# A fused spectral-mixing and SwiGLU kernel in fp32: gate and value as 4x2 by 2x4 block products with sums put into PSUM banks

## The chip, the cores and the metric

One core of one Trainium2 chip. The metric is the device time of one execution in microseconds (us). Profiled executions add a trace; engines are written PE (TensorE), PEld (its weight loads), DVE (VectorE), ACT (ScalarE), POOL (GpSimd) and SP (SyncE).

## The reference

```python
# x: (8, 3008, 256), filt_r/filt_i: (1505, 256), all fp32
X = np.fft.rfft(x, axis=1)
y = np.fft.irfft(X * (filt_r + 1j * filt_i), n=3008, axis=1)   # spectral mixing
x = y.reshape(24064, 256)
g = x @ w_gate                          # 256 -> 1536
silu = g / (1 + np.exp(-g))
out = (silu * (x @ w_val)) @ w_out      # 1536 -> 256
```

The spectral part is done as matrix products too (stages 1, 2 and 3 of a factored Fourier transform). While the hidden layer of batch b runs, the spectral stages of batch b+1 are slipped in between its products.

## The kernel before

The hidden layer is cut into 192 pieces: 8 batches, 4 chunks of tokens, 6 blocks of hidden columns. In each piece gate and value are each a 2x2 by 2x2 block product made with 7 block products in place of 8. The seven results are put together by copies out of PSUM (ACT), additions (DVE), and products that add onto a bank.

```python
def step(z, p):                         # z: gate or value, p: which of 7 products
    ...
    if p in (1, 6, 7):
        product(z, p, "A", p == 1)      # 376 columns, two records for one fp32 product
        nc.scalar.copy(out=u[(1, 6, 7).index(p)], in_=bk[z]["A"])
    ...
    elif p == 2:
        product(z, p, "F")
        add(nc.vector, dst[z][:, 0], u[0], bk[z]["F"])      # one operand in SBUF, one in PSUM
    ...                                 # (silu and multiply: cut)

e = nc.gpsimd                           # the four sums that the projection needs
add(e, h[:, 4], h[:, 1], h[:, 2])
sub(e, h[:, 5], h[:, 0], h[:, 1])
sub(e, h[:, 1], h[:, 4], h[:, 0])
sub(e, h[:, 6], h[:, 3], h[:, 1])
```

The weights of gate and value, rounded and summed once, stay in SBUF for the whole run (`wg_t`, `wv_t`).

## Time and profile before

| | before |
|---|---|
| time, median of all its runs beside the change | 3118.78 us (3118.35 to 3119.38, 4 runs) |
| profiled span | 3116.7 us |
| PE's budget (each record at its own pace) | 2992.6 us |
| loss before the first hidden product (which stands at 104.9 us) | 69.5 us |
| loss from there to 0.3 ms ("start") | 31.6 us |
| loss from 0.3 ms to 40 us before the end ("steady") | 15.5 us |
| loss in the last 40 us and after the last matmul's start ("end") | 7.4 us |

A loss is worked out from the trace like this: the distance from the start of one matmul record to the start of the next, less the pace of that form of record (0.112 us for 94 or 128 columns, 0.159 for 188, 0.216 for 256, 0.316 for 376, 0.430 for 512). It says where TensorE stood still or ran late, whatever made it. A lower granted clock is inside it. The warm-up products are not in the budget, so they count as loss before the first hidden product.

### The profile page before, as it was taken

The page shows a single profiled execution, that of the slowest core. Times are in us where ns is not written, and L with a number is a line of the kernel's source. Part 1 is how long each engine was busy: PE and PEld are TensorE (multiplying, and loading weights), DVE is VectorE, ACT ScalarE, POOL GpSimd, SP SyncE. Part 2 cuts the span into 40 slices and gives each one's busy share as a digit, 9 for nine tenths or more (in the row PEclk, how much of TensorE's full clock was granted, in tenths as well). Part 3 has the DMA queues.
Part 4 walks back from the last instruction along what each step waited for, and adds up shares of the span by engine and source line. Part 5 has one row for each costly group of instructions (what it writes and reads, how often), then busy time and mean ns, then how long its engine had stood idle before and what let it go on. Part 6 is the DMA issues. An engine that isn't in the chain of part 4 may idle for free.

```text
span 3116.7 us, 41163 instructions
## 1 busy us (share of the span) xinstructions
PE 3056.4 (98%) x15560; PEld 2240.5 (72%) x15560; DVE 1476.5 (47%) x2348; ACT 1140.3 (37%) x2070; POOL 1405.8 (45%) x1622
## 2 busy tenths in 40 slices
PE   7789999999999999999999999999999999999999
PEld 4457777777767777767777777767777677777776
DVE  4664553354543554345543455434553444544443
ACT  0443333333343343343333333343333433333333
POOL 3574454444543444444543454434544344533343
PEclk8999999999999999999999999999999999999999
DMA  8432222222212222222222132121322222200000
GB/s 233 130 117 68 72 81 56 61 76 68 75 55 72 59 79 60 61 68 81 69 60 65 57 88 71 51 71 55 91 68 56 63 63 68 68 28 21 21 6 16
DMA packets 123634, 212.51 MB, mean 68 GB/s; under 512 B 23670, under 2 KB 69750, under 8 KB 122578
## 3 DMA queue, kind: packets, MB, share of 16 engines
q1 hardware_dynamic: 91692, 132.25, 14.8%
q0 software_dynamic: 24448, 68.71, 7.7%
q10 hardware_dynamic: 7296, 8.92, 1.1%
q8 instruction: 123, 2.02, 0.3%
q14 instruction: 75, 0.61, 0.1%
HBM read 134.81 MB, written 74.97 MB: 67 GB/s over the span
## 4 chain that ended last, share of the span: by engine, by line
PE 80%; POOL 7%; DVE 6%; issue 3%; DMA 2%; ACT 2%; SPq 0%; POOLq 0%; ACTq 0%; DVEq 0%
PE wA_v L435 15%; PE wA_g L435 15%; PE wA_o L499 7%; PE wE_v L435 7%; PE wE_g L435 7%; PE wE_o L499 7%; PE wF_o L499 4%; PE wF_g L435 4%; PE pd L396 3%; PE wF_v L435 3%; POOL o L162 3%; PE pa L332 3%; POOL h L165 3%; PE pc L376 2%; PE pb L356 2%
## 5 line engine op out<-in xcount | busy, mean ns | idle before, releaser
L435 PE MATMUL wA_v<-y,wv_t 128*128 128x376 f32 x1536 | 612.5, 480 | 7.3 <-ACT u_v L444 4.3
L435 PE MATMUL wA_g<-y,wg_t 128*128 128x376 f32 x1536 | 614.3, 481 | 4.4 <-POOL wg_t L229 3.5
L165 POOL TENSOR_TENSOR h<-h 128x376 f32<-128x376 f32 x576 | 566.9, 984 | 28.8
L162 POOL TENSOR_TENSOR h<-h 128x376 f32<-128x376 f32 x192 | 188.4, 981 | 701.2 <-PE wE_v L435 389.1
L444 ACT COPY u_g<-wA_g 128x376 f32<-128x376 f32 x576 | 269.5, 468 | 589.9 <-PE wA_g L435 587.6
L435 PEld LDWEIGHTS wA_v<-y,wv_t 128*128 128x128 f32 x1536 | 289.2, 190 | 204.0 <-DVE h L457 15.6
L499 PEld LDWEIGHTS wA_o<-wo_t,h 128*128 128x128 f32 x3456 | 406.3, 192 | 16.3
L499 PE MATMUL wA_o<-wo_t,h 128*128 128x128 f32 x3456 | 417.5, 275 | 0.0
L435 PEld LDWEIGHTS wA_g<-y,wg_t 128*128 128x128 f32 x1536 | 281.1, 190 | 172.3 <-issue 28.1
L462 ACT ACTIVATE s<-s 128x1128 f32<-128x1128 f32 x192 | 219.5, 1143 | 373.2 <-DVE s L162 373.2
L464 DVE TENSOR_TENSOR h<-s,h 128x1128 f32<-128x1128 f32 x192 | 257.1, 1339 | 124.0 <-ACT s L462 124.0
L435 PE MATMUL wE_g<-y,wg_t 128*128 128x376 f32 x768 | 307.1, 482 | 2.1 <-DVE s L162 2.1
L435 PE MATMUL wE_v<-y,wv_t 128*128 128x376 f32 x768 | 306.1, 480 | 1.8 <-DVE h L162 1.6
L444 ACT COPY u_v<-wA_v 128x376 f32<-128x376 f32 x576 | 272.2, 473 | 69.3 <-PE wA_v L435 65.2
L162 DVE TENSOR_TENSOR s<-u_g,wE_g 128x376 f32<-128x376 f32 x384 | 208.9, 544 | 176.2 <-ACT u_g L444 174.6
L162 DVE TENSOR_TENSOR s<-u_g,wF_g 128x376 f32<-128x376 f32 x192 | 104.4, 544 | 394.9 <-PE wF_g L435 369.3
L499 PE MATMUL wE_o<-wo_t,h 128*128 128x128 f32 x2304 | 281.6, 276 | 7.5 <-DVE o L162 7.5
L499 PE MATMUL wF_o<-wo_t,h 128*128 128x128 f32 x2304 | 278.5, 275 | 0.0
L499 PEld LDWEIGHTS wE_o<-wo_t,h 128*128 128x128 f32 x2304 | 267.4, 192 | 13.6 <-DVE o L162 13.6
L499 PEld LDWEIGHTS wF_o<-wo_t,h 128*128 128x128 f32 x2304 | 267.8, 192 | 0.3
L162 POOL TENSOR_TENSOR p<-p,q 128x512 f32<-128x512 f32 x96 | 121.6, 1266 | 226.4 <-DVE q L367 226.4
L162 DVE TENSOR_TENSOR h<-u_v,wE_v 128x376 f32<-128x376 f32 x384 | 208.9, 544 | 26.5 <-ACT u_v L444 5.1
(86 smaller groups left out, 3275.3 us busy)
## 6 DMA issues: line engine op xcount, KB each, us to landing
t<-d SPq DMA_DIRECT2D x192, 128.0 KB
t<-d SPq DMA_DIRECT2D x64, 384.0 KB
d<-t POOLq DMA_DIRECT2D x112, 192.0 KB, 2.5
tb<-de_tbl SPq DMA_DIRECT2D x84, 256.0 KB
d<-g POOLq DMA_DIRECT2D x168, 128.0 KB, 2.8
x<-in_x_dram SPq DMA_DIRECT2D x112, 160.0 KB
out_dram<-o POOLq DMA_DIRECT2D x128, 128.0 KB, 2.0
f<-in_filt_r_dram SPq DMA_DIRECT2D x168, 64.0 KB
```

Source lines behind the costliest of these rows:

```text
L162: eng.tensor_tensor(out=dst, in0=a, in1=b, op=ALU.add)
L165: eng.tensor_tensor(out=dst, in0=a, in1=b, op=ALU.subtract)
L332: nc.tensor.matmul(out=ps[0:NK], lhsT=wf_t, rhs=self.x.pop(u), start=True, stop=True)
L356: nc.tensor.matmul(out=ps[:, i, :], lhsT=self.tb[u][:, i, 0, :], rhs=t2[:, i, :], start=True, stop=True)
L376: nc.tensor.matmul(out=ps[:, i, :], lhsT=tb[:, i, 1, :], rhs=pt[:, i, :], start=True, stop=True)
L396: nc.tensor.matmul(out=psv[:, n, :], lhsT=self.t4[k, i][:, n, ts(cb, 128)], rhs=wi_t, start=True, stop=True)
L435: nc.tensor.matmul(out=bk[z][kind], lhsT=wt[z][:, j, LEFT[p], :], rhs=y[:, RIGHT[p], :], start=start, stop=True, skip_group_check=True)
L444: nc.scalar.copy(out=u[(1, 6, 7).index(p)], in_=bk[z]["A"])
L462: nc.scalar.activation(out=s[:, 0:3], in_=s[:, 0:3], func=AF.Silu)
L464: nc.vector.tensor_tensor(out=h[:, 0:3], in0=s[:, 0:3], in1=h[:, 0:3], op=ALU.mult)
L499: nc.tensor.matmul(out=bk[kind][:, t, :], lhsT=hs[i][:, HID[p], t0:t0 + 128], rhs=wo_t[:, JB * q + i, WO[p], :], start=start and t == 0 an ...
```

## The change

Intent: TensorE is the bound, so fewer products should give a shorter run. Two former pieces become one group, 96 in all. Its gate and value are a 4x2 by 2x4 block product made with 26 products in place of 32 (28 before), of 188 columns each. What the scheme has to add up goes partly *into* PSUM ahead of a product: DVE writes a sum of two SBUF tiles into a bank and the product adds onto it. The weights no longer fit, so each group's weights come from DRAM while the group before it runs. One long list fixes the order of every operation on every engine.

```diff
-LEFT = {1: 0, 2: 1, 7: 2, 4: 3, 5: 4, 6: 5, 3: 6}
-RIGHT = {1: 0, 2: 1, 3: 2, 4: 3, 5: 4, 6: 5, 7: 6}
+SCHEDULE = """
+Q0 n1' h0' Q1 S21' f0 P3 o3' f1 t4.3' t0.0 f3 P1 x0' t0.1 P0 x1' Q2 d1 x2' c0 W1 S00' x3' c1 f2
+t0.2 x4' s01 S10' Q3 s13 x5' o1 c3 A01 A13 m01 t1.0 S31' m13 s03 S20' s23 P2 y13 t1.1 B01 t0.3 d2
+A03 u01 A23 c2 t1.2 m03 s02 B13 m23 y12 W6 u13 y23 A02 t2.0 e13 o6 e03 m02 S30' E13 t2.1 t1.3 B03
+l13 B23 u03 s12 E03 e12 y01 u23 B02 e02 l03 A12 u02 n3 t2.2 E12 m12 E02 t2.3 l12 e23 t3.0 l02 n2
+W7 t3.1 E23 o7 W2 e01 l23 g1 t3.2 E01 o2 W5 t3.3 l01 h1 t4.0 B12 o5 t4.1 W4 S01 u12 g0 W3 S11 t4.2
+o4
+""".split()
+BY_POOL = ("01", "12", "13", "23")
 ...
-    wg_t = cpool.tile([128, NJ, 7, 128], FP32)
-    wv_t = cpool.tile([128, NJ, 7, 128], FP32)
+    wt_t = cpool.tile([128, NPR, 2, 128], FP32)          # one group's 26 x 2 weight blocks
+    w_dram = wdpool.tile([NG, 128, NPR, 2, 128], FP32, name="w_all")
 ...
+    def reload_weights(g, piece):
+        a, b = PIECES[piece]
+        tc.keep_in_program_order(nc.sync.dma_start(out=wt_t[:, a:b], in_=w_dram[g, :, a:b]))
 ...
+            elif kind == "s":        # a sum put into a bank, ahead of product A
+                pin(add(v, self.bank(f"a{at}"), t[f"q{i}"], t[f"p{j}"]))
+            elif kind in "AB":       # the product adds onto it
+                self.product(op, f"a{at}", False)
+            elif kind == "y":
+                if at in BY_POOL:
+                    pin(add(nc.gpsimd, self.small(f"y{at}", 3), self.place(i, i), self.place(j, j)))
+            elif kind == "e":
+                if at in BY_POOL:
+                    pin(act.mul(self.bank(f"e{at}"), t[f"y{at}"], -1.0))
+                else:
+                    pin(negated_sum(self.bank(f"e{at}"), self.place(i, i), self.place(j, j)))
+            elif kind == "l":
+                pin(sub(v, self.place(j, i), t[f"e{at}"], t[f"m{at}"]))
+            elif kind == "S":        # sums for the projection, as before on POOL
+                h = self.hs[j]
+                dst, a, b, f = ((4, 1, 2, add), (7, 4, 0, sub), (5, 0, 1, sub), (6, 3, 7, sub))[i]
+                pin(f(nc.gpsimd, h[:, dst], h[:, a], h[:, b]))
 ...   (spectral stages cut in parts, rounding by half blocks, warm-up: cut)
```

In the list P, Q, A, B and E are products, `s` and `e` sums put into banks, `f`, `d`, `c`, `m`, `u` and `l` what leaves them, `y` and `S` sums on POOL, `g` silu, `h` the multiply, `W`, `o` and `x` the projection with its output, `n` the sums of the sequence blocks for the next group, `t` a part of a spectral stage. A prime marks work of an earlier group.

## The prediction

> **What bounds the kernel now.** I read the page's busy shares first, then TensorE's waits, then its timeline in the middle of the run.
>
> ```profile
> PE 3056.4 (98%) x15560; PEld 2240.5 (72%) x15560; DVE 1476.5 (47%) x2348; ACT 1140.3 (37%) x2070; POOL 1405.8 (45%) x1622
> ```
>
> Busy TensorE (PE) time of pipelined matmuls can hide gaps, so this alone proves little. The list of PE's waits (us in total, times, longest) is short:
>
> ```profile
> PE pc L376 <- POOL p L162: 9.2, 10, 1.8
> PE pa L332 <- DVE t L336: 8.0, 5, 3.8
> PE wE_o L499 <- DVE o L162: 7.5, 32, 0.7
> PE wA_v L435 <- ACT u_v L444: 4.3, 4, 2.7
> ```
>
> The timeline (start us, busy us, then the instruction and how many stand together) gives the pace:
>
> ```profile
> 1003.37 0.80 PE L435 MATMUL wA_v<-y,wv_t 128*128 128x376 f32 x2
> 1004.00 0.80 PE L435 MATMUL wF_v<-y,wv_t 128*128 128x376 f32 x2
> 1004.63 1.02 PE L332 MATMUL pa<-x,wf_t 94*96 94x512 f32 x2
> 1005.49 0.80 PE L435 MATMUL wA_g<-y,wg_t 128*128 128x376 f32 x2
> ```
> ```profile
> 1500.64 2.17 PE L499 MATMUL wA_o<-wo_t,h 128*128 128x128 f32 x18
> 1502.65 2.17 PE L499 MATMUL wE_o<-wo_t,h 128*128 128x128 f32 x18
> ```
>
> Each fp32 product is two matmul records. Start to start, a 376-column product takes 0.63 us (0.316 a record), a 512-column one 0.86 (0.430), and 18 projection records 2.01 (0.112 each). The 256-column records follow each other every 0.216 us, the 94-column ones (pd) every 0.112. The busy columns (0.48 us a record) overlap; only these distances count. From 0.4 ms to the end the distances have almost no excess. So PE's issue rate is the bound, and its budget is: hidden 5376 x 0.316 = 1699; projection 8064 x 0.112 = 903; spectral stages 256 x 0.430 + 768 x 0.216 + 1024 x 0.112 = 391; sum 2993 us. The other 124 us of the 3117 are mostly the first 0.3 ms, as the stage table shows (window, length, busy us of PE, PEld, DVE, ACT, POOL, clock, DMA share, GB/s):
>
> ```profile
> 55.00:95.00 40.00, 30.11 (x97) 20.93 (x98) 33.05 (x48) 6.88 (x12) 15.87 (x14) 0.80 0.59 154
> 95.00:105.00 10.00, 9.09 (x27) 4.43 (x25) 0.00 (x0) 0.95 (x2) 0.00 (x0) 0.94 0.60 160
> 105.00:165.00 60.00, 43.61 (x140) 21.75 (x141) 44.49 (x68) 30.38 (x52) 46.18 (x52) 0.94 0.42 129
> 165.00:300.00 135.00, 130.55 (x673) 94.86 (x672) 73.58 (x119) 55.34 (x102) 72.87 (x86) 0.98 0.28 85
> 1000.00:2900.00 1900.00, 1895.01 (x9794) 1404.80 (x9793) 893.23 (x1424) 710.05 (x1291) 851.39 (x978) 1.00 0.22 63
> ```
>
> The first gate product stands at 104.9 us, and weight preparation delays PE until about 0.3 ms.
>
> **What the Trainium skill says.** "TensorE: Matmul & The Clock Gate", section "Back-to-back issue gap", gives a warm distance of N/2.4 + 2.5 ns; "FP8 and Floating Point Precision", "TensorE Precision Notes", says true fp32 takes four passes. Two passes in each record give 2 x 376/2.4 + 2.5 = 315.8 ns; the trace has 316. The first page's section "LDWEIGHTS" puts a 128-column weight load at 107 ns however narrow the rest; the trace agrees in that 94 and 128 columns cost the same 112 ns. "PSUM — Partial Sum Buffer", "The four PSUM rules", says VectorE's writes do not change the bits that decide whether a matmul adds or overwrites; that is why the new kernel can put a sum in a bank and let a product add onto it, after dummy matmuls set those bits. Nothing in the kernel before shows that.
>
> **The change, part by part.**
>
> 1. Hidden products. Before, 7 for 8: 14 products of 376 columns for each of 192 pieces. After, 96 groups (each of two former pieces), with 26 products of 188 columns for both gate and value: 96 x 26 x 2 x 2 = 9984 records. The dangerous question is whether a short matmul is still paid by column. The line through 256 (216 ns) and 512 (430) gives 0.159 us at 188, clearly above the 0.112 floor, so weight loading does not bind: 9984 x 0.159 = 1590 us. This saves **109 us**. Had the floor bound them the gain would be negative, so this is the first thing to check.
> 2. Projection (8064 records) and spectral stages (same counts) stay: 0. PE's budget becomes 1590 + 903 + 391 = 2884, or 30.0 us a group.
> 3. DVE per group, from rows of before: the 376-column adds are 0.544 us, SBUF multiply 1.34 at 1128 columns, so 1.73 at 1504. Sixteen adds and subtractions on banks and halves 8.8, two multiplies 3.5, 5.7 output adds of 0.554 3.1, the sequence sums 1.7, spectral products (now three operations of 0.69 for four) 2.1, stage-3 copies 0.5: 19.7 of 30 us, 65% against 47% before. Not the bound, but far less loose.
> 4. ACT per group: 24 evictions of 0.47 = 11.3, two silus of 1.5 = 2.9, spectral copies 2.1, output copies 0.6, DMA issues 3.3 x 0.48 = 1.6: 18.5 us, 62%. POOL: 12 operations of 0.98, one addition of 1.27, two output issues of 0.58: 14.2 us, 47%.
> 5. Weights now come from DRAM for every group: 26 x 2 x 128 x 128 x 4 bytes = 3.4 MB in 30 us, 114 GB/s on top of some 65. The first 55 us moved 255 GB/s, so 180 fits. Each piece has about 20 us between its last use and its next. Hidden.
> 6. The start. In place of one column block, three or four must be ready before a group flows. All four steps of stage 3 now share one bank, each waiting for a copy of 0.8 to 1.0 us: +5 us. The third weight block is rounded behind nine sequence sums: about +11 before the third product. Then step 0 holds twelve half-roundings and six weight sums on DVE. From the before trace I estimate 2.15 us for one half (five operations, 3.56 us at double width), so 26 + 6 + the group's 11 = 43 us of DVE against 21 us of PE; step 1 has 17 + 6 + 15 = 38 against 30. Lost: 22 + 8 + 14 (with the first weights) + some 4 of friction = 48 us, against about 36 lost before at this place. First product at 112 instead of 105.
> 7. The end. The last group's multiply, five POOL sums and seven projection parts run alone: some 8 us after PE's budget is used up, 6 before.
>
> Sum: 112 to the first product, then 2884 less what of batch 0's spectral work is done by then (38) = 2846, start losses 48, end 8, and about 10 of small waits as before: 3024. To that I add 11 for new steady waits (below): **3035 us**.
>
> **Rivals.**
> (a) *The fixed order makes PE wait in every group.* Walking through the schedule with these durations, most producers finish over 1 us early. The tight place is the chain silu, multiply h0, output add, spectral products, sum s01, product A01 at the start of a group: only about 0.4 us early, and late by about 0.9 where the sequence sums n1 come first and the group begins with a spectral stage 2 (two groups of a batch, 14 us in all). For it speaks DVE at 65% in strict order; against it that the author placed everything by hand. Each 0.1 us a group costs 10 us: at 0.4 us a group the time is some 3060, at 1 us 3115 and the gain is gone.
> (b) *DVE becomes the bound.* It would need 30 us a group; I count 20. Were its operations slowed by POOL's sharing (the rounding's tensor-scalar takes 0.43 us alone and 0.70 beside POOL), it might be 23. No for the steady state, yes for the first two steps.
> (c) *Reloads collide with spectral loads* on one in-order queue, so that stage 1 or 2 waits: a few us a group at worst, 3050 to 3150. Against: the queue issues an item in 0.42 us, some 15 a group, and transfers average under 25% busy.
> (d) *The saving is bigger*, if PE has no new wait and the start is no worse: 2884 + 124 = 3008.
>
> **Range and chances.** 3005 (rival d) to 3080 (rival a at 0.6 us a group). The 2% line is 3057, 22 us above my value, i.e. 0.23 us more a group than I assume; I give 0.77 to faster, 0.21 to within 2%, 0.02 to slower.
>
> **What would show it.** Distances of 0.159 us between 188-column records confirm step 1; anything near 0.19 breaks it. PE's waits should be dominated by the first 0.25 ms; a list with hundreds of waits on DVE sums (wa) or ACT evictions means rival a; waits of spectral products on DMA mean c. DVE should read about 65% and ACT 60%; over 80% means b. The first product should stand near 112 us, and the table of stages should show PE idle for 40 to 55 us between there and 0.25 ms. The prediction is wrong if steady groups take over 30.5 us.

## More of the kernel before

The rounding of one weight block is a chain over three engines; only its shape matters here:

```python
v.tensor_scalar(out=man, in0=high, ...)                      # DVE
nc.scalar.activation(out=w, in_=man, ...)                    # ACT
v.tensor_scalar(out=pw, in0=high, ...)                       # DVE
nc.scalar.activation(out=pw, in_=pw, func=AF.Relu, ...)      # ACT
v.tensor_scalar(...); v.scalar_tensor_tensor(...); v.scalar_tensor_tensor(...)   # DVE
e.tensor_tensor(out=dst[...], in0=w, in1=pw, op=ALU.mult)    # POOL; frees w and pw
```

The DVE groups by form in the kernel before (line, engine, operation, output and inputs, shapes, count; then total busy us and mean ns; then idle time before them):

```profile
L464 DVE TENSOR_TENSOR h<-s,h 128x1128 f32<-128x1128 f32 x192 | 257.1, 1339 | 124.0 <-ACT s L462 124.0
L162 DVE TENSOR_TENSOR s<-u_g,wE_g 128x376 f32<-128x376 f32 x384 | 208.9, 544 | 176.2 <-ACT u_g L444 174.6
...
L162 DVE TENSOR_TENSOR o<-o,wF_o 128x384 f32<-128x384 f32 x64 | 35.5, 554 | 174.6 <-PE wF_o L499 161.8 <-POOL o L162 12.8
```

See what the operands are. In the second and third lines one input is a PSUM bank (wE_g and wF_o are banks, u_g and o are SBUF tiles). Only the multiply in the first line reads two SBUF tiles.

## The result

| | before | after |
|---|---|---|
| median (range, runs) | 3118.78 us (3118.35 to 3119.38, 4) | 3233.93 us (3230.89 to 3241.42, 4) |
| ratio, with 95% interval | | 1.0373 [1.0355, 1.0391], slower |
| profiled span | 3116.7 | 3229.1 |
| PE's budget | 2992.6 | 2881.3 |
| loss before the first hidden product | 69.5 | 73.4 |
| loss, start | 31.6 | 108.1 |
| loss, steady | 15.5 | 148.8 |
| loss, end | 7.4 | 17.6 |

A ratio is the mean time of one kernel's fast runs over the mean of the other's in the same rounds, so it is not quite the ratio of the medians.

The budget fell by 111 us as meant. The losses rose by 224: 77 in the start, 133 in the steady part, 10 at the end and 4 before the first product. The busy line of the changed kernel's page:

```profile
PE 2994.4 (93%) x20124; PEld 2849.8 (88%) x20124; DVE 2223.4 (69%) x3198; ACT 1568.9 (49%) x3002; POOL 1558.8 (48%) x1586
```

No engine is full, and PE fell from 98% to 93%. The pace of the new products, from TensorE's timeline in the middle of the run (start us, busy us, instruction, how many together):

```profile
1526.95 2.71 PE L584 MATMUL wa<-y_t,wt_t 128*128 128x188 f32 x16
1529.50 1.17 PE L657 MATMUL wA<-wo_t,h 128*128 128x128 f32 x9
```

Sixteen records in 2.55 us are 0.159 us each: a 188-column record is paid by its columns. So the loss is waiting. PE's waits after the change (total us, times, longest):

```profile
PE wa L584 <- DVE wa L199: 84.1, 44, 13.4
PE pa L436 <- DMA x<-in_x_dram: 25.7, 6, 5.0
PE wk L584 <- ACT q L598: 21.6, 4, 7.9
PE wpb L458 <- DMA t<-d: 16.1, 1, 16.1
```

The first line is the product onto a sum, waiting for DVE's sum: the rival (a) of the prediction, though in 44 waits and not in every group. Seven of them, 45 us, lie before 0.32 ms. The second line, six waits of about 4.3 us, is stage 1 without its input. The third is one wait early in each of the first four groups; the last of them ends at 312 us. The fourth line lies before the first hidden product. The stages (window, length, busy us of PE, PEld, DVE, ACT, POOL, clock, DMA share, GB/s):

```profile
112.00:165.00 53.00, 19.18 (x51) 13.98 (x50) 30.71 (x80) 12.32 (x30) 17.62 (x35) 0.56 0.42 139
165.00:300.00 135.00, 87.32 (x476) 78.21 (x475) 94.66 (x185) 59.91 (x123) 70.18 (x99) 0.79 0.42 137
1000.00:2900.00 1900.00, 1842.09 (x12636) 1771.28 (x12635) 1329.92 (x1850) 970.63 (x1844) 920.80 (x903) 0.99 0.57 179
```

In the first two stages no engine is busy much over 70% of the time, DVE included. That is a chain of latencies rather than a full engine. The clock there is 0.56 and 0.79 where before had 0.93 and 0.98 in the same windows; in the steady window it is 0.99 against 1.00.

The part of the loss that is the lower clock itself can be read from the traces. Take the records that follow the one before them without a wait of over 0.15 us. Those issued while the granted clock was under 0.95 stand 1.97 times their pace apart (median). From 0.32 ms to 40 us before the end, this excess makes 29 us of the loss after the change, and none before it; it is 15 us in x_early and none in s_on_dve and sum_parts, runs told below. Between the first product and 0.32 ms it makes 24 us, and 4 before the change. What lowers the clock is not shown: half_on_dve and pool_free stand idle for 111 and 100 us in the steady stretch with only 3 and 5 us of this excess.

**The sum that costs twice its price.** DVE's groups by form after the change:

```profile
L199 DVE TENSOR_TENSOR wa<-q,p 128x376 f32<-128x376 f32 x576 | 581.7, 1042 | 11.9
...
L202 DVE TENSOR_TENSOR h<-we,m 128x376 f32<-128x376 f32 x576 | 315.1, 548 | 303.1 <-PE we L584 298.9 <-ACT h L625 0.5
```

Same shape, same count. The `l` operation in the second line reads a bank and a tile and takes 548 ns, as the sums of the kernel before did. The `s` operation in the first line reads two SBUF tiles, q and p, and takes 1042 (581.7/576 gives 1.01 us). Sorted by what POOL does meanwhile, after 0.25 ms, the 148 of these sums that no POOL operation overlaps take 550 ns, and the 416 others have a median of 1291. The length goes with the number of POOL operations that overlap a sum: the medians are 812 ns beside one, 1237 beside two and 5532 beside six. The worst case, one of six such sums, in DVE's timeline and then POOL's at the same time:

```profile
1208.15 0.55 DVE L206 SCALAR_TENSOR_TENSOR p<-wk,q 128x376 f32<-128x376 f32 x1
1208.81 5.53 DVE L199 TENSOR_TENSOR wa<-q,p 128x376 f32<-128x376 f32 x1
```

```profile
1208.92 1.26 POOL L199 TENSOR_TENSOR p<-p,q 128x512 f32<-128x512 f32 x1
1210.15 0.97 POOL L199 TENSOR_TENSOR y<-h,h 128x376 f32<-128x376 f32 x1
1211.09 0.96 POOL L199 TENSOR_TENSOR y<-h 128x376 f32<-128x376 f32 x1
1212.02 0.97 POOL L202 TENSOR_TENSOR h<-h 128x376 f32<-128x376 f32 x1
1212.95 0.96 POOL L199 TENSOR_TENSOR y<-h 128x376 f32<-128x376 f32 x1
```

POOL is in the middle of an operation when the sum starts (it began at 1207.66). The sum then stays on DVE while five more POOL operations go through one behind the other, and ends 0.43 us after the last of them (1213.91 to 1214.34), somewhat less than the 0.55 that it takes alone. TensorE pays at once:

```profile
1214.49 1.12 PE L584 MATMUL wa<-y_t,wt_t 128*128 128x188 f32 x4 [2.51 <-DVE wa L199]
```

The Trainium skill has this: "SBUF — State Buffer", section "Who interferes with whom", says that a DVE instruction with two SBUF inputs contends with a GpSimd instruction that reads SBUF, that the lock is exclusive, and that who issues first decides. The trace agrees that the two contend (550 against 1291 ns). It does not show issue order deciding: five POOL operations that started after the sum went ahead of it. The prediction does not cite this page.

**Input behind the reloads.** SP's timeline, the issue of transfers in order:

```profile
930.98 39.98 SPq L323 DMA_DIRECT2D wt_t<-w_all  x7
971.01 0.89 SPq L361 DMA_DIRECT2D t<-d  x2
971.95 4.02 SPq L361 DMA_DIRECT2D x<-in_x_dram  x6
```

and TensorE's, soon after:

```profile
979.76 2.02 PE L436 MATMUL pa<-x,wf_t 94*96 94x512 f32 x2 [4.56 <-DMA x<-in_x_dram]
```

A reload may start only when the last product that reads the old block is through. SP waits for that, as the list of SP's waits says (total us, times, longest):

```profile
SPq L323 <- PE wa L584: 1368.3, 253, 10.0
SPq L323 <- PE wk L584: 592.6, 88, 16.7
```

What stands behind the reload in SP's program waits with it: x is issued at 971.95 and lands too late.

**The start.** TensorE's timeline in the first group:

```profile
133.96 5.38 PE L584 MATMUL wk<-y,wt_t 128*128 128x188 f32 x16 [5.95 <-ACT q L598]
152.46 1.62 PE L584 MATMUL wa<-y_t,wt_t 128*128 128x188 f32 x4 [13.12 <-DVE wa L199]
```

and DVE's, at the seam of two half-roundings and then at a later one:

```profile
118.75 0.43 DVE L273 SCALAR_TENSOR_TENSOR pw<-raw,pw 128x256 uint32<-128x256 uint32 x1
121.09 0.29 DVE L262 TENSOR_SCALAR w<-raw 128x256 uint32<-128x256 uint32 x1 [1.92 <-POOL wt_t L199]
...
146.72 0.29 DVE L262 TENSOR_SCALAR w<-raw 128x256 uint32<-128x256 uint32 x1 [5.47 <-DMA raw<-in_moe_w_gate_dram]
```

Each half uses the same two buffers, so DVE stands still until POOL has finished the half before (0.3 to 1.9 us, in about half of the roundings after the first product), and later until the next raw weights land. The product's sum is behind this in DVE's order.

### The profile page after: what moved, and what is told of

Its sections match the earlier page's. It is cut to its first block, busy times and chain, and to the rows that moved or that the text cites. A ratio compares the mean times of both kernels' runs of the same rounds, so it can differ in the third digit from the quotient of the medians.

```text
span 3229.1 us, 54700 instructions
## 1 busy us (share of the span) xinstructions
PE 2994.4 (93%) x20124; PEld 2849.8 (88%) x20124; DVE 2223.4 (69%) x3198; ACT 1568.9 (49%) x3002; POOL 1558.8 (48%) x1586
## 4 chain that ended last, share of the span: by engine, by line
PE 79%; DVE 11%; DMA 5%; issue 2%; POOL 2%; ACT 1%; SPq 1%; ACTq 0%; POOLq 0%; DVEq 0%
PE wa L584 22%; PE wA L657 13%; PE wk L584 11%; PE we L584 11%; PE wG L657 7%; DVE wa L199 5%; PE wF L657 4%; PE pd L506 3%; PE pa L436 3%; PE pc L486 2%; PE pb L458 2%; DMA x<-in_x_dram 1%; DMA f<-in_filt_r_dram 1%; DVE h L628 1%; DMA wt_t<-w_all 1%
## 5 line engine op out<-in xcount | busy, mean ns | idle before, releaser
L584 PE MATMUL wa<-y_t,wt_t 128*128 128x188 f32 x4608 | 858.7, 329 | 111.1 <-DVE wa L199 84.1
L584 PEld LDWEIGHTS wa<-y_t,wt_t 128*128 128x128 f32 x4608 | 757.5, 193 | 144.7 <-issue 72.5
L584 PE MATMUL wk<-y,wt_t 128*128 128x188 f32 x3072 | 573.2, 331 | 31.7 <-ACT q L598 21.6
L199 DVE TENSOR_TENSOR wa<-q,p 128x376 f32<-128x376 f32 x576 | 581.7, 1042 | 11.9
L657 PE MATMUL wA<-wo_t,h 128*128 128x128 f32 x4608 | 580.7, 276 | 5.3 <-DVE h L628 3.4
L657 PEld LDWEIGHTS wA<-wo_t,h 128*128 128x128 f32 x4608 | 564.8, 192 | 20.2 <-issue 13.2
L584 PEld LDWEIGHTS wk<-y,wt_t 128*128 128x128 f32 x3072 | 510.5, 196 | 69.8 <-ACT q L598 27.8
L584 PE MATMUL we<-y_t,wt_t 128*128 128x188 f32 x2304 | 450.0, 325 | 3.5 <-ACT we L616 2.6
L584 PEld LDWEIGHTS we<-y_t,wt_t 128*128 128x128 f32 x2304 | 376.1, 192 | 17.7 <-issue 10.9
L628 DVE TENSOR_TENSOR h<-h 128x1504 f32<-128x1504 f32 x192 | 340.9, 1776 | 69.3 <-ACT h L625 52.3
```

Of the source, the lines that this page charges most:

```text
L199: return eng.tensor_tensor(out=dst, in0=a, in1=b, op=ALU.add)
L584: pin(nc.tensor.matmul(out=ps[:, z], lhsT=wt_t[:, SLOT[p], z], rhs=rhs, start=start and z == 0, stop=True, skip_group_check=True))
L628: pin(v.tensor_tensor(out=h[:, 0:4], in0=h[:, 0:4], in1=h[:, 4:8], op=ALU.mult))
L657: pin(nc.tensor.matmul(out=self.tiles[at][:, t, :], lhsT=self.hs[i][:, HID[p], t0:t0 + 128], rhs=wo_t[:, JB * q + i, WO[p], :], start=star ...
```

## The experiments

All ratios are to the kernel before, run in the same rounds. Loss columns are those defined above, from each run's profile. One wait of 7 to 8 us, of product P1 in the fourth group for ACT's `q`, falls on the border of the two columns at 0.3 ms. It is counted as start in no_pool_sums, two_round_buffers, s_on_dve and s_on_dve_split, and as steady in after, s_two_step, x_early, no_reload, half_on_dve and dve_order. no_prepare does not have it, so it belongs to the start. With it there, after has 116 and 141, x_early 117 and 99, no_reload 116 and 106; the text below compares with these where the two sets meet.

| run | median us (range, runs) | ratio [95%] | start | steady |
|---|---|---|---|---|
| (after) | 3233.93 (3230.89–3241.42, 4) | 1.0373 [1.0355, 1.0391] | 108.1 | 148.8 |
| s_two_step | 3229.31 (3225.54–3229.62, 4) | 1.0348 [1.0331, 1.0365] | 115.6 | 138.6 |
| no_pool_sums (wrong result) | 3152.26 (3150.51–3153.18, 4) | 1.0104 [1.0089, 1.0119] | 106.1 | 72.5 |
| x_early | 3189.71 (3187.97–3190.18, 4) | 1.0224 [1.0208, 1.0239] | 108.9 | 106.8 |
| no_reload (wrong) | 3196.4 (3196.07–3199.83, 4) | 1.0247 [1.023, 1.0264] | 108.2 | 114.2 |
| two_round_buffers | 3225.28 (3217.72–3235.61, 4) | 1.0341 [1.0318, 1.0364] | 109.3 | 146.1 |
| round_ahead | 3202.01 (3201.45–3213.53, 4) | 1.0271 [1.0252, 1.029] | 89.1 | 151.5 |
| no_prepare (wrong) | 3137.18 (3131.3–3140.67, 4) | 1.0052 [1.0038, 1.0066] | 26.5 | 134.1 |
| s_on_dve | 3148.31 (3147.78–3149.13, 4) | 1.009 [1.0075, 1.0105] | 112.8 | 59.2 |
| s_on_dve_split | 3163.9 (3162.5–3166.22, 4) | 1.0141 [1.0126, 1.0156] | 111.9 | 76.6 |
| half_on_dve | 3229.79 (3226.28–3234.63, 4) | 1.0353 [1.0335, 1.037] | 110.0 | 144.5 |
| combined | 3196.84 (3191.26–3201.6, 6) | 1.0244 [1.023, 1.0258] | 89.8 | 130.5 |
| dve_order | 3221.24 (3212.39–3222.82, 4) | 1.0321 [1.0307, 1.0335] | 104.5 | 142.8 |
| best_try | 3180.27 (3168.32–3188.44, 5) | 1.0197 [1.0173, 1.0221] | 83.6 | 123.1 |
| sum_parts | 3112.38 (3108.53–3112.87, 5) | 0.9971 [0.9957, 0.9985] | 82.9 | 54.1 |
| pool_free | 3178.24 (3176.26–3180.84, 4) | 1.0186 [1.0172, 1.02] | 80.9 | 121.6 |

### s_two_step: the sum without two SBUF inputs

```diff
-                pin(add(v, self.bank(f"a{at}"), t[f"q{i}"], t[f"p{j}"]))
+                a = self.bank(f"a{at}")
+                pin(act.copy(out=a, in_=t[f"q{i}"]))
+                pin(add(v, a, a, t[f"p{j}"]))
```

> Correct result. The sum q+p that DVE puts into a bank reads two SBUF tensors and takes 1.04 us in the mean, 0.55 where no POOL operation overlaps it. Here ACT first copies q into the bank and DVE adds p to it in place, so DVE reads only one SBUF tensor; POOL's work is unchanged, ACT gains 576 copies of about 0.48 us. Theory A (DVE's second SBUF read waits for POOL's running operation): the 576 additions fall to 0.55 us each, PE's waits on these sums after 0.3 ms fall from about 80 us to under 20, the time to 3130 to 3175 us. Rival B (the fixed order is simply too tight, or a DVE write to PSUM is slow by itself): they stay near 1 us or PE's waits stay, and the time stays within 1% of 3234, or rises because ACT has more to do.

Right result. The sum's row by form:

```profile
L199 DVE TENSOR_TENSOR wa<-wa,p 128x376 f32<-128x376 f32 x576 | 302.0, 555 | 539.6 <-ACT wa L605 539.6
```

With one operand in PSUM the same sum, beside the same POOL work, takes 555 ns. So the place of the operands makes its length; that is shown. The time hardly moved, so the 3130 to 3175 us that were expected are missed. The likely reason is the row's last part, which is new: DVE stands idle 540 us in all for ACT's copy, a step more in the same chain. After 0.32 ms TensorE's waits for these sums fell from 39 to 14 us, but waits before the same products that the list puts down to TensorE itself rose from 3 to 20.

### no_pool_sums: the POOL work taken away

```diff
             elif kind == "y":
-                if at in BY_POOL:
-                    pin(add(nc.gpsimd, self.small(f"y{at}", 3), self.place(i, i), self.place(j, j)))
+                pass
 ...
-                    pin(act.mul(self.bank(f"e{at}"), t[f"y{at}"], -1.0))
+                    pin(act.mul(self.bank(f"e{at}"), self.place(i, i), -1.0))
 ...
-                pin(f(nc.gpsimd, h[:, dst], h[:, a], h[:, b]))
+                pass
```

> Wrong result on purpose. POOL's twelve additions and subtractions of a group are left out (the recombination of the hidden values, and the sums that ACT negates into a bank); ACT reads one of the two summands instead. DVE, ACT and PE keep all their instructions. Theory A: DVE's sums fall to 0.55 us, its 1504-column multiply to 1.72, and the loss of PE after 0.3 ms falls from 149 us to some 40 to 60 (what remains is the wait for x and small ones): 3110 to 3145 us. Rival B: sums near 1 us, time over 3200.

The sums still read two SBUF tiles:

```profile
L199 DVE TENSOR_TENSOR wa<-q,p 128x376 f32<-128x376 f32 x576 | 329.0, 604 | 14.5 <-ACT q L598 1.4 <-ACT h L602 0.6
```

They fall to 604 ns, and the steady loss halves, from 141 to 72.5 us (the border wait taken out of both). The time is 7 us over the range expected. This is a limit for what POOL's presence costs and not a pure price of the lock, since the run also takes away the chain from POOL's `y` over ACT's `e` to product E.

### x_early and no_reload: the input behind the reloads

x_early issues the first three x tiles of a batch two groups earlier, ahead of the reloads; no_reload leaves the weights as they stand after the first groups.

```diff
+                if b + 2 < B and (step, op) == (10, "Q3"):
+                    load_x_early(b + 2)          # x_early (the helper is cut)
```
```diff
-                if op in ends and not last and (b or step > 1):
+                if op in ends and not last and False:          # no_reload
                     reload_weights((g + 1) % NG, ends[op])
```

> Correct result. Only the first three x tiles of the batch after next are loaded one group of three earlier than the group that needs them (in the eleventh group of a batch instead of the first of the next). Theory: in the first group of each batch PE waits some 5 us for x, 29 us in six batches, because the load stands in the one in-order queue behind weight reloads that wait for PE's last products of the group before; with the loads early the wait goes and the time falls by 20 to 30 us, to about 3207. Rival: the queue or the transfers are merely slow, the wait moves to the next load (second stage or later x) and the time falls by under 10.

> Wrong result on purpose. The weights are not reloaded after the first two groups (every later group multiplies with what is there); all else stays. It tests the rival that the 320 MB of reloads and their places in the in-order queue cost time: if only the x loads suffer, the time falls by about as much as with the early x, 35 to 50 us; if the reloads also slow other transfers or products that wait for weights, by over 60; the sums on DVE stay at about 1.04 us.

x_early takes what stage 1 loses by waiting for x from 29 us, as the losses count it (25.7 in the list of waits), to 0.3, and the steady loss from 148.8 to 106.8. Of these 42 us, 14 are records at a lower clock (29 to 15). The time fell by 44 us, more than the 20 to 30 expected. no_reload gains no more (114.2), and leaves the sums at 1069 ns. So the reloads cost time through the order of issue on SP; their 114 GB/s of traffic costs nothing that these runs can show. x_early is 7 us ahead of no_reload; TensorE's waits for the sums are longer in no_reload (104.2 us in 58, against 84.3 in 45), and why is not explained.

### two_round_buffers, round_ahead and no_prepare: the start

```diff
-        pw = rpool.tile([128, 2, 128], U32, name=f"pw_{i}", tag="pw")           # two_round_buffers
-        w = rpool.tile([128, 2, 128], FP32, name=f"w_{i}", tag="w")
+        pw = rpool.tile([128, 2, 128], U32, name=f"pw_{i}", tag="pw", bufs=2)
+        w = rpool.tile([128, 2, 128], FP32, name=f"w_{i}", tag="w", bufs=2)
```
```diff
-    START = 6                                # round_ahead: the above, and
+    START = 8
 ...
-            raws[i] = p.tile([128, 2, 128, 2], U32, name=f"raw_{i}", tag="raw", bufs=2)
+            raws[i] = rpool.tile([128, 2, 128, 2], U32, name=f"raw_{i}", tag="raw", bufs=4)
 ...
-            load_weights(i + 1, nc.scalar, True)
+            load_weights(i + 3, nc.scalar, True)
```
```diff
-            prepare = PREPARE.get(step, {}) if b == 0 else {}      # no_prepare
+            prepare = {}
 ...   (every reload takes group 0's weights; the projection's weights are a constant)
```

> Correct result. Rounding a weight half uses two buffers for its two work tiles instead of one (and three instead of four product tiles in the first batch to make room). Theory C (the start loses 108 us because each half is a serial chain DVE, ACT, DVE, POOL on a single buffer: DVE waits about 1.6 us for POOL before each next half, 36 halves): the loss between the first product and 0.3 ms falls by 20 to 40 us. Rival D (DVE's or POOL's busy time, or the arrival of the raw weights, sets the pace): under 10 us, waits for the raw weights take the place.

> Correct result. The changed kernel with two work buffers for the rounding, as before without success (the wait for POOL turned into waits for the raw weights of 1 to 5 us), and now also four buffers for raw weights, loaded three halves ahead instead of one. Theory C' (a chain of rounding latencies paces the start): the loss between first product and 0.3 ms falls from 108 to 65 to 85 us, time to about 3195 to 3210. Rival D' (in the first two groups DVE's fixed order, in which roundings stand between a product's evictions and the next sum, is what PE waits for whatever the buffers): it stays above 95.

> Wrong result on purpose. The changed kernel with no rounding or combining of weights after the first group's own: all groups use the first group's weights, reloaded as before, and the projection a constant. Theory (the 108 us lost between the first product and 0.3 ms are DVE's, ACT's and POOL's weight work standing in the fixed order between a product and the next sum): the loss falls to 20 to 40 us, of which some 20 come before the first group's weights are ready. Rival (a cold clock of TensorE, or the filling of the pipeline of groups, costs by itself): it stays over 60.

(Both rounding runs need one buffer less for the spectral products of batch 0, for space.) A second pair of buffers alone does little for the start: 109.3 for 116, the border wait in both. DVE's waits for POOL before a rounding are almost gone (2.0 us in all, where the changed kernel has 23.1), and its waits for raw weights have doubled (22.3 us for 10.9), with 1.65, 5.42, 1.14 and 1.36 us in the first groups. With the raw weights loaded three ahead as well, the start falls from 116 to 89.1, which just misses the 65 to 85 expected, and the median by 32 us. The profiled run was the slowest of its four, and its steady loss is 11 us higher than the 141.

no_prepare does no rounding beyond the first group's own weights. Its start on TensorE:

```profile
134.32 5.38 PE L584 MATMUL wk<-y,wt_t 128*128 128x188 f32 x16 [6.03 <-ACT q L598]
140.33 1.54 PE L584 MATMUL wa<-y_t,wt_t 128*128 128x188 f32 x8 [0.63 <-DVE wa L199]
```

The wait of 13.12 us for the sum is 0.63, and the start's loss is 26.5. Preparing weights beside the first groups therefore makes 90 of the 116 us; the wait for ACT of 6 us just before stays, so it is another matter.

### s_on_dve and s_on_dve_split: the projection's sums on DVE

```diff
-                pin(f(nc.gpsimd, h[:, dst], h[:, a], h[:, b]))       # both, on x_early
+                pin(f(v, h[:, dst], h[:, a], h[:, b]))
-A01 A13 m01 t1.0 S31' m13 s03 S20' s23 P2 ...      (the other six S stood elsewhere)
+A01 A13 m01 t1.0 m13 s03 s23 S00' S01' S10' S11' P2 ...  l03 S20' S21' ...  o7 S30' S31' ...
```
```diff
-Q0 n1' h0' ...                                      # s_on_dve_split, on top
+Q0 n1b' h0' ...  n2 n1a ...  o2 n1e ...
```

> Correct result. On top of the early x (3190 us): the eight recombinations of a group go from POOL to DVE (about 0.55 us each, so DVE gets 4.4 us more, some 24 of 30 us a group), at places of the fixed order where the products that need them are still far. POOL keeps four sums of 0.98 us. The ACT-copy experiment took the lock away but put a hop in its place and won 5 us; leaving POOL's sums out won 76 us after 0.3 ms. Theory A: with most of POOL's reads gone and no hop added, DVE's q+p sums fall from 1.04 to about 0.6 us and the loss after 0.3 ms from 107 to 40 to 60 us: 3125 to 3150 us. Rival B: DVE is now too full for its fixed order, PE's waits on DVE stay above 60 us: 3170 us or more.

> Correct result. As the run with the recombinations on DVE, and of the three sums of neighbouring sequence blocks (2.2 us of DVE at the start of every third group, just ahead of the multiply) two are done earlier in the group before. Theory: in those groups the chain silu, multiply, spectral products, s01, A01 is about 1.5 us shorter; the waits at the first sums' products in groups 3, 6 and 9 of a batch fall, 10 to 25 us in all against the run without the split. Rival: these waits were the lock's, gone already: within 5 us.

DVE has 768 more operations and the kernel is faster, with the right result. The sum's row in x_early, and then here:

```profile
L199 DVE TENSOR_TENSOR wa<-q,p 128x376 f32<-128x376 f32 x576 | 589.5, 1056 | 11.9
L199 DVE TENSOR_TENSOR wa<-q,p 128x376 f32<-128x376 f32 x576 | 327.6, 601 | 15.3 <-ACT h L613 1.5 <-ACT q L609 1.4
```

The steady loss goes from 99 to 59.2 and the time falls by 41 us. This is the strongest evidence for the lock, since here POOL is relieved by giving DVE more to do. That POOL's S sums were themselves late for TensorE is no rival: in x_early it waited for them once, for 1.2 us. The order was changed in the same edit, and its part was not separated. The second edit, meant to take two of the sequence sums off the start of a group, cost 16 us. The wait of projection part 3 grew from 14 to 29 us. It was dropped.

### half_on_dve, combined, dve_order and best_try: orders that were thought better

half_on_dve puts only S0 and S1 on DVE and keeps S2 and S3 on POOL, with an order made for it; dve_order keeps all four on DVE, in an order meant to spread them; both also put o5 ahead of h1 (not in the cuts below), which sum_parts does too; combined and best_try are these two with round_ahead.

```diff
-                pin(f(nc.gpsimd, h[:, dst], h[:, a], h[:, b]))           # half_on_dve, on x_early
+                pin(f(v if i < 2 else nc.gpsimd, h[:, dst], h[:, a], h[:, b]))
+... m03 s02 S00' S01' S10' S11' B13 m23 e13 y12 u13 y23 S20' S21' A02 t2.0 e03 m02 E13 W6 S30' S31' ...
```
```diff
-... s23 S00' S01' S10' S11' P2 ... s02 B13 m23 y12 W6 u13 y23 A02 t2.0 ... l03 S20' S21' ... W7 t3.1 E23 o7 S30' S31' W2
+... s23 S00' S01' P2 ... s02 S10' S11' B13 m23 y12 u13 y23 A02 W6 t2.0 ... l02 S20' S21' n2 W2 t3.1 E23 o2 W7 ... o7 S30' S31'
```

> Correct result. The early x, and a second order for the recombinations: of the eight of a group the four that come first go to DVE just after the sum s02, the other four stay on POOL after its sums y; projection part W6 moves behind E13, and the output addition o5 comes before the multiply h1. In the run with all eight on DVE (3148 us, 59 us lost after 0.3 ms) the waits that were left were at A02 (17 us), at W3 (14, for o5 behind h1) and at stage-2 matmuls (17, DVE full). Theory: places alone are at fault there; the loss after 0.3 ms falls to 30 to 45 us and the time to 3115 to 3138. Rival (POOL's four again block DVE's sums s12, e02, e03): the loss stays at 60 or more, 3150 us.

> Correct result. The run before with the deeper buffers of the rounding (which alone took the start's loss from 108 to 89 us). If the parts add up, the time is 18 to 25 us below the run before: 3095 to 3118 us, faster than or level with the kernel before the change. If not, the start's gain is lost in later waits.

> Correct result. All eight recombinations on DVE with the early x, as in the run that took 3148 us, with five places of the fixed order changed: o5 before the multiply h1, two recombinations after s02 instead of before it with W6 behind A02, two later ones behind l02 with W2 and W7 exchanged. The mixed order of two runs ago, with four recombinations left on POOL, lost 144 us after 0.3 ms because POOL's runs again held up DVE (its negated sums took 1.25 us); with POOL out, theory: only places matter, the waits at A02, W3 and stage 2 (48 us together) fall by half, time 3120 to 3135. Rival: DVE at some 80% has no room in groups with three stage-2 pieces; the waits only move and the time stays above 3140.

> Correct result. The run before with the deeper rounding buffers. If the gains add, 18 to 25 us below it: 3098 to 3117 us, level with the kernel before the change (within 2%), perhaps just below it; whether it beats it at all is open.

All four missed. Against s_on_dve, dve_order moves no work between engines and is 73 us slower (3221.24 to 3148.31). In half_on_dve and dve_order a new wait stands high among PE's waits, for S sums that the projection needs. In half_on_dve it is

```profile
PE wA L668 <- DVE h L202: 45.2, 53, 2.1
```

and in dve_order

```profile
PE wA L668 <- DVE h L202: 29.7, 46, 2.1
```

In s_on_dve this wait is 3.2 us, in 2 times. In half_on_dve DVE's own S subtractions take 1.14 us and its `e` sums 1.24 on average, both with two SBUF inputs, so the lock is back there in other operations. In dve_order it hardly is: the s sums take 610 ns, about as in s_on_dve, and the S subtractions 0.67 us for 0.56. Its steady loss from 0.32 ms is 75 us above that of s_on_dve, 37 of them in waits of over 0.15 us, 26 at a lower clock and 12 in shorter delays. In half_on_dve the shares of the lock and of the order were not separated. round_ahead is worth 33 us on half_on_dve and 41 on dve_order, about as much as alone.

### sum_parts and pool_free: the parts that held, and POOL emptied further

```diff
-... t3.3 l01 h1 t4.0 B12 o5 t4.1 W4 ...       # sum_parts: s_on_dve, round_ahead, and
+... t3.3 l01 o5 h1 t4.0 B12 t4.1 W4 ...
-BY_POOL = ("01", "12", "13", "23")            # pool_free: on top of that
+BY_POOL = ()
```

> Correct result. The best order so far (all recombinations on DVE, early x: 3148 us) with the deeper rounding buffers and one move alone, the output addition o5 ahead of the multiply h1, which W3's wait of 14 us points at. If the causes found add up (POOL in DVE's way, x behind the reloads, the rounding chain), the time is 3110 to 3125 us and within 1% of the kernel before. If moving anything in this order costs as much as it did in the last two orders: 3140 or more.

> Correct result. As the run with the parts together, and POOL's last four sums of a group are left out too: DVE writes the negated sum into the bank for all six pairs instead of two, so DVE has 2.2 us more a group, some 26 to 27 of 30, and POOL only one addition of a spectral stage. Theory A alone (contention is what counts): DVE's sums go to 0.55 us and the time falls by 5 to 20 us. Rival B (DVE's load now counts): the time rises by 20 us or more against the run with the parts together.

sum_parts gives the right result in 3112.38 us, ratio 0.9971 [0.9957, 0.9985]: it beats the change by 122 us and the kernel before by 0.3%. Its busy line, two of PE's waits, and the sum's row:

```profile
PE 2957.3 (95%) x20124; PEld 2826.9 (91%) x20124; DVE 2344.9 (75%) x3966; ACT 1562.6 (50%) x3002; POOL 745.8 (24%) x818
```
```profile
PE wa L594 <- DVE wa L199: 25.7, 7, 9.7
...
PE pc L496 <- DVE q L487: 13.4, 20, 1.0
```
```profile
L199 DVE TENSOR_TENSOR wa<-q,p 128x376 f32<-128x376 f32 x576 | 335.9, 615 | 14.8 <-ACT q L608 1.4 <-ACT h L612 0.5 <-DVE p L206 0.5
```

POOL fell to 24%, the waits for sums from 44 to 7, the sum to 615 ns. pool_free shows where this ends. With all `y` and `e` sums on DVE too, the s sums stay at 606 ns, but the run is 66 us slower, and the first of PE's waits is a new one:

```profile
PE we L594 <- DVE we L206: 49.1, 47, 2.9
```

Now products E wait for DVE's own queue. Moving the S sums paid; moving these four `e` sums a group as well did not, as the expectation's rival B had it.

## Why the prediction was wrong, point by point

- **Step 1 (the pace of 188 columns): right.** 0.159 us, and the budget is 2881 for a predicted 2884 (9984 x 0.159 is 1587, not 1590). The weight loads that it sets beside the 112 ns are records of 192 ns each that overlap, so 107 ns is not seen as such. That a product adds onto DVE's sum in a bank, which the kernel before could not show, is borne out by the right results of x_early, s_on_dve and sum_parts.
- **Step 2 (projection and spectral counts): right**, as the same budget shows. **First product: right**, 111.4 us for 112.
- **Step 3 is the step that failed in size.** Its term "Sixteen adds and subtractions on banks and halves 8.8" prices each at 0.544 us, from rows whose operands are a tile and a bank. Eight of the sixteen read two tiles. The six `s` sums took 1.01 us on average, which is (581.7/576 - 0.544) x 576 = 268 us more DVE work; the two `e` sums took 0.65. The share of DVE hides this (69% for a predicted 65%); what counts is that these sums stand directly ahead of products in a fixed order. Taking POOL's sums away brings the steady loss down by 68 us (no_pool_sums, which takes away a chain as well); moving the S sums away from POOL, by about 40 (s_on_dve against x_early). The sign that the prediction set itself came: groups 24 to 83 took 31.6 us on average, over its 30.5.
- **Rival (a) named the place, rival (b) the mechanism.** Product A01 "only about 0.4 us early" is where PE waited: 21 us at A01, and 38 at A13 just behind it, with 20 more at A02. It expected hundreds of waits, and there were 44. POOL's sharing was seen, in the rounding's 0.43 and 0.70 us, and then waved off for the steady state ("it might be 23", "No"). It was weighed as DVE load where it should have been weighed as lateness of one operation.
- **Step 5 ("Hidden") failed for x.** The bandwidth was right and the traffic harmless (no_reload). The queue was not: six waits of 4.3 us on average, and 42 us of steady loss that x_early removed. Rival (c) said this, at "a few us a group at worst"; it was six groups, not ninety-six.
- **Step 6 (the start) was mis-sized**: 48 us predicted, 108 measured, or 116 with the border wait. The 43 us of DVE against 21 of PE are busy time. The rounding is a chain DVE, ACT, DVE, POOL on one pair of buffers with raw weights one ahead, so DVE spent as much time waiting as working: in the first stage it was busy 30.7 of 53 us. no_prepare confirms the cause (90 of the 116 us); two_round_buffers and round_ahead suggest that each link hides the next.
- **Step 4**: right in the main. ACT's 49% for 62% is no error of that size: the 1.6 us of DMA issues are not busy time in the profile and a group was longer, so it is some 16 us a group for 16.9. POOL is some 15 us for 14.2, its sums 1.09 us for 0.98. **Step 7**: 17.6 us at the end for 8; no run tested it. Two slips of adding: rival (a) at 1 us a group is 3024 + 96 = 3120, not 3115, and rival (d) is 3008, where the range begins at 3005.

The account closes: 111.4 to the first product, 2881.3 less 38 of budget done by then, then losses of 108.1, 148.8 and 17.6 make 3229, the profiled span. Against the predicted terms the start is 60 over, the steady part 128 over (21 were allowed), the end 10; with the border wait in the start, 68 and 120.

Still open: about 83 us in the start and 54 in the steady part of sum_parts, the end, what lowers the clock, and why the two hand-made orders cost as much as they did.

## What to carry to other kernels

Price a new instruction from a row with the same kinds of operands, not only the same shape: two SBUF inputs on VectorE beside a busy GpSimd are another price than one SBUF and one PSUM input, and in a fixed order the longest case counts, not the mean. When a saving on the bounding engine is bought with more work and traffic elsewhere, ask of each new producer how late it may be, and of each queue what stands behind a wait in it. Change an order only with a run at hand: here a reordering that moved no work between engines cost 73 us, where the whole change cost 115.

## What the Trainium skill lacked or had wrong

- "SBUF — State Buffer", "Who interferes with whom": right on two-input DVE instructions beside GpSimd (550 against 1291 ns), but it speaks of one instruction blocking one other. With GpSimd operations queued back to back, one DVE sum was held over one that was running and five that started after it, 5.53 us. That longest case is what a fixed order has to plan for.
- "TensorE: Matmul & The Clock Gate", "Back-to-back issue gap": no spacing for fp32 records. Measured: 0.112 us at 94 and 128 columns, 0.159 at 188, 0.216 at 256, 0.316 at 376, 0.430 at 512. An estimate from the page's isolated formula, with two passes in each record, gives the ones from 188 up to within 1 ns or so; the sustained 131 ns that it sets beside the formula at 512 columns is not seen here (430 ns for two passes).
- I found no page that says this outright: a transfer whose issue waits for an engine holds every later transfer in the same issuing engine's program. SP waited 1368 us for `wa` and 593 us for `wk` products ahead of reloads, and TensorE waited 4.3 us on average for x in six batches.
